# Shorter key blocks without the middle copy of the global keys, and another order of the first steps, in a banded attention with a gated MLP

## The chip, the cores and the metric

The kernel runs on one core of a Trainium2 chip. Its engines are TensorE (PE, with PEld for its weight loads), VectorE (DVE), ScalarE (ACT) and GpSimd (POOL); SyncE (SP) issues all DMAs of this kernel, in order. The metric is the device time of one execution in microseconds, as the median of several runs; durations come from one profiled execution.

## The reference

There are 8 batches of 8 heads, 512 local and 32 global tokens, 64 channels per head, all in float32. The output is cut to this:

```python
s_g = scale * q_g @ k_all.T                 # global tokens see every key
out_g = softmax(s_g) @ v_all
s_ll = where(abs(i - j) <= 32, scale * q_l @ k_l.T, -1e9)
s_l = concat([scale * q_l @ k_g.T, s_ll])   # local: 32 global keys and a band
out_l = softmax(s_l) @ concat([v_g, v_l])
x = rows of concat([out_g, out_l])          # 8 * 544 rows of 512
out = (((x @ w1) * (x @ w2)) @ w3) @ w_out  # no activation between
```

## The kernel before

**Attention.** Of a head's 512 queries, four blocks e of 128 are scored against a window of keys: `WIN` gives where a window begins in the loaded keys and how wide it is, `PAT` where its probabilities stand in the row `P` of the head (`PW` wide). In the loaded row of keys (`KD` = 608 wide) the 32 global keys g stand between the blocks of 128 local ones, three times: k0 g k1 g k2 g k3. A middle window (256 wide) holds 32 keys of the block before, g, 128 of its own, g again, and 32 of the next; one of the two g is masked out. Heads go in pairs: one head's keys lie in partitions 0 to 63 and the other's in 64 to 127, and `scores` issues their products alternately on the two halves of the array (a block's product shows as two matmuls in the trace). `scores1` does the heads 0 and 1 singly. `minus_max` adds the mask and takes the row minimum of the negated scores on DVE, `exps` the exponential on ACT.

**Two ways to turn the probabilities.** For heads 0 to 7 PE transposes them (`transposes`), ACT and DVE copy them into `PT` and `G`, and float32 products follow. From head 8 on DVE turns 32 by 32 squares (`turn` for the edges and global columns, `turn_own` for the own keys), and the squares are put in place through DRAM: `own_out` writes the tile `od`, `own_in` reads it back as `own` in four DMAs (there is one buffer for `own`, free again when the head before has been split), `weights_hi` rounds it into `PT` (ACT PT<-own) and `weights_lo` subtracts (PT<-own,PT). `move_out` and `move_in` do the same for the columns of G. Then `values` makes the products av with the values, in halves x.

**MLP.** The weights come packed, so that DVE (shift L841, merge L845) and ACT (scale L843) unpack them. w3 and w_out are first multiplied with each other on PE (`fold`, 8 times 8 products of 512 columns, L921 `w<-wo,w3f`), which makes w34. w1 and w2 are split into high and low parts; the second half of them, named w12s in the steps, comes in 16 pieces through three buffers, and a piece's fetch (SP L885) waits until the low part (DVE or POOL, `w12l`) of the piece three before it is made. `first` makes ap and bp (24 matmuls of 256 columns for two blocks m), `gate_a` copies ap out on ACT (`as`, L793), after which ap's one bank may be written again, `gate_b` multiplies on DVE, `second` adds to the output accumulators (acc, 6 matmuls per m).

**Order.** A list `PLAN` of some 3,880 entries gives every step's number and its engine (P, A, D, V for POOL, S); each engine works through its own entries in order and waits at the first whose inputs or buffers are not there. A few dummy products (`IDLE`) fill PE at the start.

Of the kernel before, what the change touches and what calls it, by code (L numbers as in the profile page):

```python
# [20 lines left out]
KD = 608  # L21
WIN = [(0, 192), (96, 256), (256, 256), (416, 192)]
PAT = [0, 192, 448, 704]
PW = 896
# [6 lines left out]
def i(ap):  # L31
# [8 lines left out]
    qgl=(250, 461), vgh=606, vgl=(620, 1290), mmax=(437, 502), exps=(545, 592), inv=350, mul=(420, 740),  # L40
    hi=(587, 231, 231, 475, 294, 203, 256), hi_dve=(683, 260, 260, 540, 0, 0, 292), lo=(692, 253, 253, 559, 540, 247, 280), half=(470, 530), sum=520, join=485,
# [4 lines left out]
    scores1=1650, scores2=1910, ownt=780, ownl=(691, 1300), values32=(1180, 1130), gscores32=930, take=(446, 521), shiftp=(330, 300, 420),  # L46
# [24 lines left out]
    1V 790S 386S 3V 328S 791S 0S 390S 329S 8S 12S 16S 389S 5V 387P 792P 152S 846S 388D 793D 391P 795D 794A 797D 796A  # L71
    392D 798A 9D 393A 799D 10A 394D 800A 11D 395P 14A 13D 801P 20S 396A 397A 15D 802D 24S 18A 813P 845S 803D 804D 17D
    19D 805A 808A 806A 248P 807V 814D 816D 28S 809P 815A 399S 817A 158S 818D 820D 811P 819A 821A 22A 21D 825P 830A 23D
    826D 249P 32S 164S 827A 829A 828A 847P 822D 832A 810D 26A 823S 25D 27D 36S 900S 831V 812D 30A 258P 868D 848D 850D
    833P 835P 849A 852D 854D 853A 851A 29D 31D 398S 250P 863A 855A 862V 870D 40S 872D 400P 403S 874D 34A 33D 856P 834A
    875A 251P 166A 873A 836D 35D 44S 857A 259P 260P 837D 859D 869A 858D 7V 401D 899S 261P 861A 38A 860D 37D 864P 866P
    39D 871A 48S 876D 877S 42A 165D 167D 41D 865A 879P 43D 886A 885A 404P 52S 880D 884A 881A 330S 883A 262P 405D 882A
    46A 2V 887P 45D 406A 47D 252P 888A 56S 407D 824S 901P 953S 50A 49D 253P 902D 51D 867A 889P 54A 53D 60S 331A 55D
    903A 159D 254P 922D 924D 58A 64S 57D 255P 256A 59D 263P 264P 265P 890A 68S 257D 268P 269P 923A 891V 402S 154A 839V
    904D 906D 892V 270P 908D 408P 160A 842V 266A 267D 333A 62A 61D 878S 909A 925A 271P 63D 272P 332D 72S 65D 66A 843A  # L80
    67D 409A 273P 926D 76S 410A 928D 70A 278P 69D 71D 929A 274P 907A 844D 80S 917A 275P 153D 412S 893V 279P 276D 277D
    954S 280P 74A 73D 281P 905A 75D 84S 927A 282P 896D 78A 910P 77D 930D 931S 283P 284P 912D 911A 79D 933P 915A 914A
# [12 lines left out]
    1031A 441D 1020A 1005A 1000V 419A 421A 3091P 1058D 1021V 420V 3095A 1057D 1114D 3093P 184A 422D 1229S 1061A 183D
    185D 1033S 172A 3092P 3094P 3101P 3102P 186A 171D 173D 178A 1059S 177D 1022A 187D 174A 179D 450S 1018A 175D 180A
    1084D 1085A 1086D 200S 1088D 1087A 188S 1116D 1115A 3096D 1089A 1062V 1065S 1019V 1023V 434S 1006V 3097A 1118D
    1034P 1037P 1060S 1120D 1090D 1035A 3103P 181V 3098D 202A 1038A 201D 1053V 1036D 1055A 194S 190A 3104P 1064V 1056V
    1039D 3105A 189D 191D 1091A 1066S 442P 203D 3111P 3106D 1156S 192A 1063A 1054V 1051A 1050S 193V 206S 1098D 451A
    1052D 3099P 204A 452V 1117A 1102A 1099D 196A 1067P 1070P 205D 1068A 1100S 3100P 218S 195D 197D 1094A 1071A 1103D  # L100
    198A 1095V 1069D 1106S 3113P 435A 199D 3107A 436V 1072D 212S 208A 3112P 3108D 437A 1101S 443A 207D 209D 1119A 3109P
    444D 438V 220A 1121A 219D 221D 1107S 1157P 210A 1122D 1104A 211V 1132D 1133S 1105A 1131D 1073V 1096A 222A 213D 214A
    3114P 224S 1135A 223D 1123S 3115A 215D 236S 1158D 1136V 1097V 3110P 1092A 1093V 1188D 216A 1190D 1139S 1159A 1160D
    1108P 217V 466S 1191A 3116D 1161A 1134S 3117A 1078V 1111P 1162D 1163A 1164D 1192D 3123P 3118D 226A 1194D 445S 1138A
    1165A 1137V 1140S 1109A 1112A 3121P 225D 237D 227D 228A 1075V 230S 1129A 229V 1172D 1176A 1110D 1113D 1127A 1177V
    242S 1173D 453P 454A 455D 1125A 1130V 1180S 1128V 238A 1174S 1126D 456A 1124S 239D 1141P 1144P 1189A 457D 458D
# [12 lines left out]
    3165P 1222V 486S 1293D 1328S 1323S 3166P 344A 1291D 473A 474V 1294D 1326A 1343A 1354D 1295V 3160D 1296V 3154P 475A
    1344D 1327A 1355S 1345S 494A 3161V 487S 1379P 3169A 1297D 3162V 3167P 1380D 1382D 1314V 1353D 3168P 1383A 1329S  # L120
    1315V 1410D 1381A 1412D 1357A 3163P 1414D 1411A 1416D 1298A 1358D 1318A 1299V 3179P 1384D 1361S 1386D 1385A 1227A
    1356S 1319V 3181P 345D 1316A 476D 3180P 3182P 1387A 1317V 3164P 1300V 1395D 504S 488S 495V 3170D 1301A 1396S 1330P
    1333P 1331A 3183P 3187A 1362S 1359V 1334D 1417A 1228D 3184P 1347V 1332D 3132S 3185P 3186P 1525S 3171A 1335D 1349A
# [161 lines left out]
def band_attention_glu_kernel(  # L285
# [20 lines left out]
    nc = tc.nc  # L306
# [6 lines left out]
    S = 544  # L313
# [12 lines left out]
    ident = cs[:, 0:128]  # L326
# [14 lines left out]

    def constants():
        nc.sync.dma_start(cs, cst)

    T = {}
    M = {}

# [180 lines left out]
    def transposes(n):  # L528
        P = Ps[n % NP_]
        tt = T["tt", n] = ps_1.tile([128, 2, 4, 128], F32, tag="pu", name=f"t{n}", bufs=2)  # L530
        for e in range(4):
            nc.tensor.transpose(tt[:, 0, e, :], P[:, 256 * e : 256 * e + 128], ident)
# [931 lines left out]
```

## Time and profile before

| | us |
|---|---|
| median of 3 runs (809.15 to 809.78) | 809.75 |
| the profiled execution | 809.29 |
| its span, first to last instruction | 807.5 |
| PE busy | 794.4 |
| DVE, ACT, POOL busy | 531.2, 455.3, 390.9 |
| PE in the chain that ended last | 94% of the span |

The page cuts the span in 40 slices; PE stands at 9 tenths or more in all but two of them, at about 117 and 147 us. A busy PE in this profile means that some matmul is in flight; since matmuls overlap, what one costs is read from how far apart they start, which is what the chain of work shows.

### The profile page before, as it was taken

Reading aid. Unit: us, or ns where it says so; the run is one execution under the profiler, and the core shown is the slowest. Engines: PE = TensorE matmul, PEld = TensorE weight load, DVE = VectorE, ACT = ScalarE, POOL = GpSimd, SP = SyncE. Lnnn points to the kernel's source line nnn. Section 1 sums busy time; section 2 is a strip of 40 time slices with the busy share of each in tenths; the row PEclk is TensorE's granted clock in tenths of the full one; section 3 lists DMA queues with packets and bytes.
Section 4 is the critical chain, followed back from the end, with each engine's and each line's share of the span. In section 5 each row is a group of like instructions: output and inputs, shape, how many; then the busy total and the mean of one; then the engine's idle time right before and its main releaser. Section 6 shows DMA issues by size and latency. Waiting matters only on the chain.

```text
span 807.5 us, 17227 instructions
## 1 busy us (share of the span) xinstructions
PE 794.4 (98%) x5608; PEld 704.6 (87%) x5608; DVE 531.2 (66%) x1504; ACT 455.3 (56%) x1290; POOL 390.9 (48%) x603
## 2 busy tenths in 40 slices
PE   9999989799999999999999999999999999999998
PEld 7656568699999999999999999999998999999997
DVE  4877978878777666677688867666576587612111
ACT  4767877776555545466665757665566554412011
POOL 1122354666555657656546556546556565412110
PEclk9999999999999999999999999999999999999999
DMA  8887877866557457565666656666664555300000
GB/s 275 266 267 226 262 193 193 207 171 187 160 151 206 122 155 180 144 188 138 162 174 170 202 157 169 177 171 173 187 171 130 137 152 153 97 27 14 15 27 26
DMA packets 191554, 128.85 MB, mean 160 GB/s; under 512 B 114472, under 2 KB 151592, under 8 KB 191464
## 3 DMA queue, kind: packets, MB, share of 16 engines
q1 hardware_dynamic: 191464, 127.75, 57.7%
q8 instruction: 44, 0.72, 0.4%
q14 instruction: 46, 0.38, 0.1%
HBM read 92.73 MB, written 34.96 MB: 158 GB/s over the span
## 4 chain that ended last, share of the span: by engine, by line
PE 94%; DVE 2%; ACT 1%; DMA 1%; SPq 1%; issue 0%; POOL 0%; ACTq 0%; DVEq 0%; POOLq 0%
PE bp L787 8%; PE ap L787 8%; PE acc L821 8%; PE acc L820 8%; PE acc L819 8%; PE bp L788 7%; PE bp L789 7%; PE ap L788 7%; PE ap L789 7%; PE w L921 7%; PE av L636 7%; PE s L491 6%; PE av L630 2%; PE sg L686 2%; DMA own<-od 1%; PE idle L364 1%
## 5 line engine op out<-in xcount | busy, mean ns | idle before, releaser
L787 PE MATMUL bp<-x,w12h 128*128 128x256 f32 x544 | 153.0, 281 | 0.0
L787 PE MATMUL ap<-x,w12h 128*128 128x256 f32 x544 | 152.5, 280 | 0.0
L788 PE MATMUL bp<-x,w12h 128*128 128x256 f32 x544 | 151.0, 278 | 0.0
L789 PE MATMUL bp<-x,w12l 128*128 128x256 f32 x544 | 150.8, 277 | 0.0
L788 PE MATMUL ap<-x,w12h 128*128 128x256 f32 x544 | 150.6, 277 | 0.0
L789 PE MATMUL ap<-x,w12l 128*128 128x256 f32 x544 | 150.5, 277 | 0.0
L504 ACT ACTIVATE P<-P,small 128x256 f32<-128x256 f32 (+1 forms) x256 | 121.6, 476 | 25.9 <-DVE small L500 25.1
L787 PEld LDWEIGHTS ap<-x,w12h 128*128 128x128 f32 x544 | 102.1, 188 | 4.0 <-issue 2.9
L787 PEld LDWEIGHTS bp<-x,w12h 128*128 128x128 f32 x544 | 102.6, 189 | 3.3 <-issue 2.2
L788 PEld LDWEIGHTS bp<-x,w12h 128*128 128x128 f32 x544 | 102.7, 189 | 0.7
L788 PEld LDWEIGHTS ap<-x,w12h 128*128 128x128 f32 x544 | 102.3, 188 | 0.7
L789 PEld LDWEIGHTS bp<-x,w12l 128*128 128x128 f32 x544 | 102.6, 189 | 0.0
L789 PEld LDWEIGHTS ap<-x,w12l 128*128 128x128 f32 x544 | 102.2, 188 | 0.0
L500 DVE CUSTOM_DVE_ANT_0 P<-s,cs 128x192 f32<-128x192 f32 (+1 forms) x256 | 86.1, 383 | 7.1 <-PE s L491 4.2
L650 DVE TENSOR_TENSOR u<-av,cb 64x352 f32<-64x352 f32 x112 | 55.7, 517 | 33.3 <-ACT cb L417 30.9
L417 ACT COPY cb<-av 64x352 f32<-64x352 f32 x71 | 30.6, 446 | 61.3 <-PE av L636 46.8
L636 PE MATMUL av<-PT,vs 128*128 128x192 f32 x448 | 62.0, 266 | 0.6 <-POOL PT L420 0.6
L921 PE MATMUL w<-wo,w3f 128*128 128x512 f32 x128 | 58.7, 597 | 0.3 <-DVE wo L845 0.3
L491 PEld LDWEIGHTS s<-kq,qp 64*128 64x128 f32 x496 | 43.3, 186 | 15.6 <-issue 6.5
L420 POOL TENSOR_TENSOR TT<-TT 128x352 fp32r<-128x352 f32 x38 | 38.5, 1013 | 35.7 <-ACT TT L417 20.5
L491 PE MATMUL s<-kq,qp 64*128 64x192 f32 (+1 forms) x496 | 55.4, 362 | 0.0
L636 PEld LDWEIGHTS av<-PT,vs 128*128 128x128 f32 x448 | 53.0, 164 | 2.7 <-POOL PT L420 0.8
(818 smaller groups left out, 1872.5 us busy)
## 6 DMA issues: line engine op xcount, KB each, us to landing
od<-tw SPq DMA_DIRECT2D x56, 256.0 KB, 2.6
own<-od SPq DMA_DIRECT2D x224, 64.0 KB, 2.4
raw_w<-in_w_t_dram SPq DMA_DIRECT2D x24, 512.0 KB, 4.9
kq<-in_kd_t_dram SPq DMA_DIRECT2D x32, 304.0 KB, 3.6
kpr<-in_kp_t_dram SPq DMA_DIRECT2D x32, 272.0 KB, 3.9
out_dram<-o_None SPq DMA_DIRECT2D x33, 256.0 KB, 2.8
qp<-in_q_t_dram SPq DMA_DIRECT2D x32, 256.0 KB, 3.7
R<-rd SPq DMA_DIRECT2D x64, 128.0 KB, 3.1
```

The source lines that it names most:

```text
L491: nc.tensor.matmul(st[:, x, c : c + w], q[r, 128 * e : 128 * e + 128], k[r, o : o + w], start=(e % 2 == 0), stop=True, skip_group_check=True)
L500: nc.vector.tensor_tensor_reduce(blk(n, e), s, masks[e], -0.125, 3.0e38, ALU.add, ALU.min, T["mn", n][:, e : e + 1])
L504: nc.scalar.activation(blk(n, e), blk(n, e), AF.Exp, bias=T["mn", n][:, e : e + 1], scale=-1.0, accum_out=T["sm", n // 2][:, n % 2, e : e ...
L636: nc.tensor.matmul(av[0:r, o : o + 32 * (s1 - s0)], v[:, 0:r], PT[:, s0:s1, y, j], start=False, stop=(j % 2 == 1 and (plain or y == 1)), s ...
L650: nc.vector.tensor_add(T["u", n // 2][r : r + 64, x], T.pop(("av", n, x))[r : r + 64, 0:352], T["cb", n][r : r + 64, x])
L787: nc.tensor.matmul(d, wh[:, k, c, :], x[:, 0, 0:w], start=(k == m % 2 == 0), stop=False, skip_group_check=True)
L788: nc.tensor.matmul(d, wh[:, k, c, :], x[:, 1, 0:w], start=False, stop=False, skip_group_check=True)
L789: nc.tensor.matmul(d, wl[:, k, c, :], x[:, 0, 0:w], start=False, stop=(k == 3), skip_group_check=True)
L819: nc.tensor.matmul(a, gh[:, m % 2, sl], wh[:, c], start=(m == 0), stop=False, **part)
L820: nc.tensor.matmul(a, gh[:, m % 2, sl], wl[:, c], start=False, stop=False, **part)
L821: nc.tensor.matmul(a, gl[:, m % 2, sl], wh[:, c], start=False, stop=(m in (5, 7)), **part)
L921: nc.tensor.matmul(T["w34", t], T["w3f", t, j // 4][:, j % 4], T["wo"][:, j], start=(j == 0), stop=(j == 7))
```

## The change

The keys are loaded without the copy of g between k1 and k2: k0 g k1 k2 g k3, in one DMA of two pieces of 288 columns. The windows become 192, 224, 224 and 192 wide, each with g once, at another place in the last two than in the first two. All that reads `P` follows: the columns of `transposes`, the squares of `turn` and `turn_own`, the pieces copied to G. The constant masks are the same array, in which a new step on POOL (`masks`, two copies of 128x32) exchanges two strips before the first masked block is read. In `values` the second of two value blocks takes its 64-column product first. The order of the first 1,378 of the 3,877 entries is new (to about head 16); the rest of the list is as it was.

```diff
-KD = 608
-WIN = [(0, 192), (96, 256), (256, 256), (416, 192)]
-PAT = [0, 192, 448, 704]
-PW = 896
+KD = 576
+WIN = [(0, 192), (96, 224), (256, 224), (384, 192)]
+PAT = [0, 192, 416, 640]
+PW = 832
...
-    1V 790S 386S 3V 328S 791S 0S 390S 329S 8S 12S 16S 389S 5V 387P 792P 152S 846S 388D 793D 391P 795D 794A 797D 796A
+    1V 790S 386S 328S 3V 387P 791S 792P 0S 3877V 388D 390S 793D 8S 391P 5V 794A 795D 392D 797D 799D 796A 393A 12S 800A
...
-    masks = [cs[:, 384:576], mask, mask, mask[:, 0:192]]
+    masks = [cs[:, 384:576], cs[:, 128:352], cs[:, 352:576], cs[:, 128:320]]
...
+    def order_masks():
+
+        nc.gpsimd.tensor_copy(cs[:, 320:352], cs[:, 352:384])
+        nc.gpsimd.tensor_copy(cs[:, 352:384], cs[:, 128:160])
...
-        nc.sync.dma_start(kr, kd_t[b, 2 * p : 2 * p + 2].rearrange("h d s -> (h d) s"))
+
+        k = kd_t[b, 2 * p : 2 * p + 2].rearrange("h d s -> (h d) s")
+        nc.sync.dma_start(kr.rearrange("p (a s) -> p a s", a=2), view(k, 0, [320, 2], [1, 288]))
...
-        nc.vector.transpose(view(t, 32, [256, 3], [64, 3], [1, 32]), view(P, 160, [32, 3], [256, 3], [1, 32]))
-        nc.vector.transpose(t[:, 7, 1], P[:, 128:160])
+        nc.vector.transpose(view(t, 32, [256, 2], [64, 3], [1, 32]), view(P, 160, [32, 2], [224, 3], [1, 32]))
+        nc.vector.transpose(view(t, 480, [64, 2], [128, 2], [1, 32]), view(P, 128, [96, 2], [448, 2], [1, 32]))
...
-            for y in range(1 if plain else 2):
+            ys = (0,) if plain else (1, 0) if j % 2 else (0, 1)
+            for y in ys:
...
-                [("s", n) if n < 2 else ("sp", n // 2), *([("mmax", n, e - 1)] if e else [("load", "cs")])], minus_max, n, e)
+                [("s", n) if n < 2 else ("sp", n // 2), *([("mmax", n, e - 1)] if e else [("masks",)])], minus_max, n, e)
...
+    add(("masks",), only("POOL", 200, True), -30.0, [("load", "cs")], order_masks)
```

**DVE, after the last fold.** Here DVE makes the last low part of w34 and then the low parts `w12l` of the first three w12s pieces. Before:

```order
L928 TENSOR_TENSOR w34l_998<-w_7_948,w34h_997 128x512
L658 COPY u_896<-av_7_989 64x352
L509 TENSOR_SCALAR sums<-sums 128x8
L510 RECIPROCAL sums<-sums 128x8
L420 TENSOR_TENSOR w12l_1016<-raw_w12s_2_266,w12h_1015 128x256
L420 TENSOR_TENSOR w12l_1016<-raw_w12s_0_150,w12h_1015 128x256
L662 TENSOR_TENSOR u_896<-u_896 128x32
L663 TENSOR_TENSOR u_896<-u_896 128x32
L526 TENSOR_TENSOR u_896<-u_896,R_951 128x256
L420 TENSOR_TENSOR w12l_1016<-raw_w12s_1_240,w12h_1015 128x256
```

The same place now:

```order
L936 TENSOR_TENSOR w34l_991<-w_7_911,w34h_990 128x512
L666 COPY u_890<-av_7_968 64x352
L426 TENSOR_TENSOR w12l_1002<-raw_w12s_2_638,w12h_1001 128x256
L426 TENSOR_TENSOR w12l_1002<-raw_w12s_0_185,w12h_1001 128x256
L426 TENSOR_TENSOR w12l_1002<-raw_w12s_1_206,w12h_1001 128x256
L426 TENSOR_TENSOR x_2_0_946<-u_665,x_2_0_946 128x256
```

The three low parts now follow each other, and the sums (`inverse`) and the work on u stand behind them.

**ACT, at the first copy of ap.** `as` is the copy that frees ap's bank; raw_w12s is a piece of weights just fetched, TT the turned edges of a head. Before:

```order
L417 CAST x_3_1_1098<-u_896 128x256
L417 CAST vs_1102<-vr_1006 128x4x64 x2
L793 COPY as__1119<-ap_0_0_1056 128x512
L843 ACTIVATE raw_w12s_1_1042<-raw_w12s_1_1042 128x256
L417 CAST TT<-TT 128x11x32
L843 ACTIVATE raw_w12s_3_1054<-raw_w12s_3_1054 128x256
```

And now:

```order
L423 CAST vs_1085<-vr_1034 128x4x64
L851 ACTIVATE raw_w12s_1_1037<-raw_w12s_1_1037 128x256
L423 CAST TT<-TT 128x11x32
L801 COPY as__1101<-ap_0_0_1054 128x512
L851 ACTIVATE raw_w12s_3_1040<-raw_w12s_3_1040 128x256
```

The copy has moved behind the scale of the first fetched piece and behind TT. On PE the second `first` of ap has moved the other way: before, 24 matmuls on bp stood between the first ap and the next, now 12 do, and the other 12 come after it, ahead of head 8's values.

**PE, ahead of head 11's values.** sg are scores of global queries, av the values, acc the accumulators. Before:

```order
L787 MATMUL ap_0_6_1560<-x_3_0_1075,w12h_1019 128x256
L788 MATMUL ap_0_6_1560<-x_3_0_1075,w12h_1019 128x256
L789 MATMUL ap_0_6_1560<-x_3_0_1075,w12l_1020 128x256
L686 MATMUL sg_1594<-kph_1318,QG_423 128x272 x2
L686 MATMUL sg_1594<-kpl_1330,QG_423 128x272 x2
L630 MATMUL av_1616<-G_1039,vgs 128x288
```

And now:

```order
L694 MATMUL sg_1570<-kph_1309,QG_420 128x272 x2
L694 MATMUL sg_1570<-kpl_1358,QG_420 128x272 x2
L827 MATMUL acc_0_0_1299<-w34h_779,gh__1529 128x512
L828 MATMUL acc_0_0_1299<-w34l_780,gh__1529 128x512
L829 MATMUL acc_0_0_1299<-w34h_779,gl__1546 128x512
L827 MATMUL acc_0_128_1300<-w34h_779,gh__1529 128x512
L828 MATMUL acc_0_128_1300<-w34l_780,gh__1529 128x512
```

One `second` (6 matmuls) that stood behind head 11's values now stands ahead of them; 12 matmuls of a `first` have changed places with the global scores.

## Rows read from the trace of the kernel before

**Rows 1.** The page, part 1: busy time, share, instructions of each engine.

```profile
PE 794.4 (98%) x5608; PEld 704.6 (87%) x5608; DVE 531.2 (66%) x1504; ACT 455.3 (56%) x1290; POOL 390.9 (48%) x603
```

**Rows 2.** Windows: length, busy PE, PEld, DVE, ACT, POOL, granted clock, DMA, GB/s.

```profile
105.00:125.00 20.00, 17.21 (x127) 16.18 (x126) 14.91 (x47) 14.72 (x43) 11.54 (x16) 0.91 0.84 203
...
140.00:160.00 20.00, 15.21 (x100) 12.86 (x99) 17.01 (x57) 15.52 (x46) 13.88 (x24) 0.91 0.87 213
...
200.00:300.00 100.00, 100.00 (x759) 92.74 (x758) 71.15 (x198) 54.46 (x161) 57.15 (x89) 1.00 0.60 161
```

**Rows 3.** PE's waits over the span: us in total, times, longest.

```profile
PE av L630 <- DVE small L717: 3.8, 1, 3.8
PE av L630 <- ACT P L504: 2.8, 1, 2.8
...
PE av L636 <- POOL PT L420: 0.6, 1, 0.6
PE av L630 <- ACT w12h L417: 0.4, 1, 0.4
```

**Rows 4.** The chain that ended last: start, us, what.

```profile
7.46 1.71 PE s L476 x8
...
79.18 6.87 PE w L921 x16
...
155.88 1.72 PE s L491 x16
```

**Rows 5.** Groups by form: count, busy us, mean ns of one.

```profile
L636 PE MATMUL av<-PT,vs 128*128 128x224 f32 x112 | 31.3, 280 | 0.0
...
L636 PE MATMUL av<-PT,vs 128*64 128x224 f32 x112 | 30.3, 270 | 0.0
```

**Rows 6.** The chain from the last fold to head 8's values.

```profile
105.95 0.60 DVE w34l L928
...
107.23 0.39 DVE sums L509
...
109.27 0.34 DVE w12l L420
...
109.63 0.33 SPq L885
...
110.05 0.97 SPq L556
...
112.78 5.26 DMA own<-od
...
118.14 0.62 ACT PT L417
...
120.48 0.40 PE av L630
```

**Rows 7.** DVE in order of time, 100 to 134 us.

```profile
107.77 0.71 DVE L420 TENSOR_TENSOR w12l<-raw_w12s,w12h 128x256 fp32r<-128x256 f32 x2
...
127.35 0.65 DVE L420 TENSOR_TENSOR PT<-own,PT 128x512 fp32r<-128x512 f32 x1
...
131.75 0.53 DVE L650 TENSOR_TENSOR u<-av,cb 64x352 f32<-64x352 f32 x1 [1.06 <-ACT cb L417]
132.31 0.43 DVE L420 TENSOR_TENSOR w12l<-raw_w12s,w12h 128x256 fp32r<-128x256 f32 x1
```

**Rows 8.** POOL in order of time, 118 to 121 us.

```profile
118.83 1.27 POOL L420 TENSOR_TENSOR PT<-own,PT 128x512 fp32r<-128x512 f32 x1 [2.55 <-ACT PT L417]
120.18 0.24 POOL L420 TENSOR_TENSOR G<-TGg,G 32x32 fp32r<-32x32 f32 x1
```

**Rows 9.** ACT in order of time, 112 to 115 us.

```profile
112.29 0.59 ACT L793 COPY as__1119<-ap 128x512 f32<-128x512 f32 x1 [0.36 <-PE ap L789]
114.45 0.45 ACT L843 ACTIVATE raw_w12s<-raw_w12s 128x256 f32<-128x256 f32 x1 [1.57 <-DMA raw_w12s<-in_w_t_dram]
114.79 0.47 ACT L417 CAST TT<-TT 128x352 fp32r<-128x352 f32 x1
```

**Rows 10.** Tile bp, 108 to 117.5 us: ns min/median/max, first and last start.

```profile
L787 PE MATMUL bp<-x,w12h x8: 276/276/276, 112.1 to 114.5; 128*128 128x256 f32 x8
```

**Rows 11.** The chain at a `second`, one of its six.

```profile
128.02 0.23 PE acc L819
```

**Rows 12.** SP's waits over the span.

```profile
SPq L885 <- DVE w12l L420: 6.2, 4, 3.2
```

More of the change, by code (lines that the diff above doesn't have):

```diff
@@ L39 @@
     kh=703, kl=(790, 1500), qh=617, ql=(620, 1290), vh=404, vl=(545, 746), kph=647, kpl=(726, 1374), qgh=298,
-    qgl=(250, 461), vgh=606, vgl=(620, 1290), mmax=(437, 502), exps=(545, 592), inv=350, mul=(420, 740),
-    hi=(587, 231, 231, 475, 294, 203, 256), hi_dve=(683, 260, 260, 540, 0, 0, 292), lo=(692, 253, 253, 559, 540, 247, 280), half=(470, 530), sum=520, join=485,
+    qgl=(250, 461), vgh=606, vgl=(620, 1290), mmax=(437, 470), exps=(545, 568), inv=350, mul=(420, 740),
+    hi=(587, 231, 231, 366, 294, 203, 366), hi_dve=(683, 260, 260, 416, 0, 0, 416), lo=(692, 253, 253, 559, 540, 247, 280), half=(470, 530), sum=520, join=485,
     joing=750, xh=405, xl=(411, 740), cg=610, mg=790, eg=840, ng=820, wg=(683, 292), ga=588, gb=691, gh=620,
@@ L45 @@
     gtrans=465, own=355, turn=650, gturn=1010, edge=(513, 520), edgel=(520, 960), first=1372, second=1382, fold=860,
-    scores1=1650, scores2=1910, ownt=780, ownl=(691, 1300), values32=(1180, 1130), gscores32=930, take=(446, 521), shiftp=(330, 300, 420),
+    scores1=1543, scores2=1610, ownt=780, ownl=(691, 1300), values32=(1180, 1130), gscores32=930, take=(446, 521), shiftp=(330, 300, 420),
 )
@@ new lines @@
+    430D 132A 952D 973A 431D 133V 1009P 1010D 140S 136A 318P 313P 135D 1012D 137D 314P 993V 315P 1014D 1155S 975A 141D
+    146S 319P 167D 142A 1011A 432S 138A 1082S 1015A 1040D 1013A 320P 148A 1016D 321P 439S 1042D 948A 316A 139V 1081S
+    322P 147D 1230S 323P 149D 143D 317D 324P 150A 1017A 325P 1024D 995P 986S 1044D 1025D 151V 144A 145V 1041A 1028A
+    433S 326A 1029V 1046D 1043A 327D 168A 1026S 1032S 162A 997P 156V 996D 6V 1083P 169D 418S 157D 182S 163D 170S 4V
+    998A 949D 1047A 440A 999D 1045A 1022A 1001D 3087P 1002A 1031A 176S 1030A 441D 1023V 1020A 3089P 1058D 419A 1003V
@@ new lines @@
+    184A 3088P 1084D 1057D 1061A 1004V 183D 3090P 3095A 1027S 1059S 1033S 1048D 185D 171D 1062D 172A 173D 1114D 3091P
+    3092P 3101P 186A 1005A 187V 1086D 1116D 174A 421A 1018A 175V 1021V 1118D 1088D 420V 1120D 1065S 200S 3102P 188S
+    1117A 1087A 1019D 3093P 178A 1049S 1119A 3094P 1085A 177D 1229S 179D 1006V 3096D 1090D 1115A 1089A 1034P 180V 1037P
+    201D 1035A 3097A 3103P 181D 189D 1038A 1036D 1060S 422V 3104P 1064V 190A 1039D 1063A 194S 1091A 191D 1055A 450S
+    3098D 1053A 1000V 1099D 1098D 442P 1056V 192A 1054V 1066S 202A 1051A 193D 195D 1052D 3105A 3099P 196A 1102A 451A
@@ new lines @@
+    1379P 3162D 1328S 474D 1297V 1327A 3170D 495V 1380D 3179P 3181P 3163P 1298A 1382D 1381A 1227A 1315D 1355S 1384D
+    1299V 3164P 1386D 1353D 487S 1410D 1357A 1329S 475A 3171A 1412D 345V 1318A 1316A 1358V 1300D 1383A 1387A 1319V
+    1385A 1317V 3183P 1228D 3172D 1395D 1356S 3180P 3185P 3182P 1414D 3187A 1296V 1330P 1333P 3132S 3173P 1351A 1331A
+    3193P 1332D 1359V 3184P 1361S 1411A 1360V 1396S 1334A 3186P 1394D 476V 1362S 1398A 1349A 3194P 1415A 488S 1347V
+    1416D 1352D 1348D 1350V 1345S 1301A 1335D 496P 1399V 3188D 1417A 1363P 1366P 1451S 3174P 3195P 1364D 1413A 3197A
@@ new lines @@
+    1365D 1452S 1402S 1367A 1368D 1400A 1397S 1390A 504S 1302V 497A 3189A 489A 1428D 1401V 3177A 3175A 498D 1429S 1391D
+    1392A 490V 1427D 1431A 1526S 3203P 1403S 491A 3190D 1346S 1393D 1418D 1453P 1454D 1388A 1432V 3204P 1484D 505A
+    1455A 3196P 1456D 1486D 346S 1457A 1458D 1488D 1389V 1460D 1461A 3198D 492V 3191P 1404P 1459A 1487A 1407P 1435S
+    506V 1369V 1405A 1490D 3205P 1469D 1408A 507P 1406D 1419S 1423A 1409D 3192P 1425A 3207A 1371V 1374D 3206P 508A
+    1375A 1430S 3213P 1485A 1433V 1470S 1434V 1424V 1436S 1421A 3199A 509D 1525S 510A 1426V 1468D 1422D 3200D 499S 511D
@@ new lines @@
+    1437P 1489A 1472A 1420S 1471S 1372A 512D 1473V 3214P 1491A 1440P 1438D 1441A 513S 1502D 1439D 1442D 500V 1443V
+    3201P 3208D 1475V 1476S 1474A 3202P 1527P 1492D 1528D 501V 3215P 1462A 1445V 1503S 1501D 1530D 3217A 347A 514S
+    3216P 1532D 1558D 3209A 1505A 3210V 1463V 1506V 1464V 1466A 3218D 1534D 1560D 1467D 3227P 1373D 1562D 3228P 3211P
+    1564D 1370V 1531A 1477S 1493S 3212P 1535A 3231A 1504S 1448D 1509S 1465V 1376D 1533A 348V 1529A 1543D 3178S 520S
+    1494S 1478P 3219V 1481P 1479D 1510S 1508D 3220V 1480D 1499A 1482D 502A 1544S 3176S 349A 3229P 1507A 3230P 1495A
@@ L137 @@
+    503V 1483D 1542D 1561A 1446A 1500V 3221P 515S 1497A 521A 1496D 3232D 1599S 531S 1559A 3222P 1498D 522D 1511P 1546A
+    1449A 1547D 1514P 3225D 3233V 3234V 1550S 3237P 1545S 1512D 1513D 1600S 1540A 1565A 1515A 1538A 3238P 350D 523P
     1673S 1516D 1548A 3226S 3223D 1517V 3241A 3239P 1551S 1450D 1519V 1563A 532A 1549A 516V 518V 1576D 3240P 1536V 524A
@@ L326, in band_attention_glu_kernel @@
     ident = cs[:, 0:128]
-    mask = cs[:, 128:384]
-    masks = [cs[:, 384:576], mask, mask, mask[:, 0:192]]
+    masks = [cs[:, 384:576], cs[:, 128:352], cs[:, 352:576], cs[:, 128:320]]
     Ps = [const.tile([128, PW], F32, tag=f"P{e}", name=f"P{e}") for e in range(NP_)]
@@ L530, in transposes @@
         tt = T["tt", n] = ps_1.tile([128, 2, 4, 128], F32, tag="pu", name=f"t{n}", bufs=2)
-        for e in range(4):
-            nc.tensor.transpose(tt[:, 0, e, :], P[:, 256 * e : 256 * e + 128], ident)
-        for e in range(3):
-            nc.tensor.transpose(tt[:, 1, e, :], P[:, 256 * e + 128 : 256 * e + 256], ident)
+        for e, c in enumerate((0, 256, 448, 704)):
+            nc.tensor.transpose(tt[:, 0, e, :], P[:, c : c + 128], ident)
+        for e, c in enumerate((128, 352, 576)):
+            nc.tensor.transpose(tt[:, 1, e, :], P[:, c : c + 128], ident)
     def turn(n):
         P, t = Ps[n % NP_][:], f(TT[:])
-        nc.vector.transpose(view(t, 32, [256, 3], [64, 3], [1, 32]), view(P, 160, [32, 3], [256, 3], [1, 32]))
-        nc.vector.transpose(t[:, 7, 1], P[:, 128:160])
+        nc.vector.transpose(view(t, 32, [256, 2], [64, 3], [1, 32]), view(P, 160, [32, 2], [224, 3], [1, 32]))
+        nc.vector.transpose(view(t, 480, [64, 2], [128, 2], [1, 32]), view(P, 128, [96, 2], [448, 2], [1, 32]))
     def turn_own(n):
@@ L545, in turn_own @@
         t = T["tw", n] = p1.tile([128, 512], F32, tag="tw", name=f"tw{n}")
-        nc.vector.transpose(view(t[:], 0, [32, 4], [128, 4], [1, 32]), view(P, 0, [256, 4], [32, 4], [1, 32]))
+        nc.vector.transpose(view(t[:], 0, [64, 2], [32, 2], [128, 4], [1, 32]), view(P, 0, [448, 2], [256, 2], [32, 4], [1, 32]))
     def own_out(n):
@@ L597, in pieces @@
         tt = T["tt", n]
+        g_own = G[0:32, 32:S].rearrange("g (c d x) -> g c d x", c=2, d=2)
         if e == 0:
```

109 lines of the change are left out of this document (41 added, 68 removed).

## The prediction

> **What bounds the kernel now.** I read the busy times first: PE is busy for 794.4 of 807.5 us, the next engine, DVE, for 531.2 [rows 1]. The windows say where the rest is: from 200 to 300 us PE is busy in 100 of 100 us at full clock while DVE has 29 us to spare [rows 2], so there only PE's own work counts. [...] The waits name the places: PE stands 2.8 us ahead of head 8's values, 1.0 us around head 10's and 3.8 us ahead of head 11's [rows 3]. So up to 7.6 us of standing and 3.6 us of lost clock lie within the stretch whose order is new, and everywhere else the kernel is as long as PE's matmuls. The last view is the chain, for what a matmul costs and for who is late at those places.
>
> **Part 1, narrower score blocks.** 16 fold matmuls of 512 columns take 6.87 us in the chain [rows 4], 0.84 ns a column. The score matmuls of a pair of heads are 8 steps, the two heads side by side: 4 steps of 192 and 4 of 256 columns, 1,792 columns, 1.50 us by that price; the chain has 1.72 [rows 4], the rest being the ends. Now the four wide steps have 224 columns: 4 x 32 x 0.84 ns = 0.107 us less. There are 31 such pairs, and the heads 0 and 1, scored singly with the same 8 steps each (1.71 us [rows 4]), save as much each: 33 x 0.107 = 3.5 us, nearly all of it where PE never waits, or ahead of a chain that starts on PE. Ends of the price: 0 if the steps are not set by columns (a rival below), 3.5 if they are; I take 3.5, since the fold row prices a column.
>
> The trace shows both heads' 16 matmuls in 1.72 us and one head's 8 in 1.71 [rows 4]: twice the weight loads, the same time. [...]
>
> **Part 2, the order at head 8.** The chain there [rows 6, 7]: the last low part of w34 at 105.95, the sums at 107.23, two low parts w12l (0.71 us from 107.77), a third at 109.27, by which the third fetch leaves at 109.63 and the read-back of head 8's own keys only at 110.05; it lands at 118.04, is rounded on ACT at 118.14 (0.62), and its low part takes POOL 1.27 us, with G's 0.24 behind it [rows 8]. In the new order the three low parts follow each other: 107.23 + 0.71 + 0.34 = 108.28 instead of 109.61, 1.3 us earlier for the read-back. The low part of the own keys goes to DVE, 0.65 us [rows 7], with G's part done before: 118.76 + 0.65 = 119.4 instead of 120.4, 1.0 less. Seven score blocks ahead of it take off 0.75. So the operands stand at 120.5 - 1.3 - 1.0 - 0.75 = 117.4, and PE comes at 117.7 - 0.75 = 116.9: this wait shrinks to about 0.5 us.
>
> What is late next is the copy that frees ap's bank. It ran at 112.29, ahead of the scale of the first fetched piece, which waited for its DMA until 114.45 [rows 9]. Now it stands behind that scale (0.45) and TT's rounding (0.47). The first fetch can leave 0.6 us earlier (the sums no longer ahead) and all is 0.75 earlier, so the piece lands at about 113.1, and the copy ends near 113.1 + 0.8 + 0.6 = 114.5. PE wants the bank after 12 instead of 24 matmuls on bp, which run from 112.1 to 114.6 [rows 10]: at 113.35 - 0.75 = 112.6. It would stand 1.9 us there, then has 36 matmuls left (4.1 us at the pace of rows 10) and is at head 8's values at 118.6 instead of 120.5. Behind the copy on ACT stand the next piece's scale and, five steps on, head 8's rounding; at 114.5 that still waits for its data. Gain 1.9, of which 0.75 is in part 1: 1.2 us. Ends: -1 if the piece lands no earlier, +2.4 if the copy isn't late.
>
> **Part 3, the order at heads 10 and 11.** The read-back of head 10 waits for a fetch, and that for a low part at 132.31, which stood behind a sum that waited 1.06 us and took 0.53 [rows 7]. The new order puts this low part first: 1.6 us earlier, and the one buffer of `own` hands that on to head 11. One `second`, six matmuls of 0.23 us [rows 11], now runs ahead of head 11's values, 1.4 us of work where PE stood 3.8. Together 3.0 us at most. Against it: a low part of the gate that this `second` needs has gone from DVE to POOL, which for the same 512 columns takes 1.27 against 0.65 us [rows 7, 8], and PE arrives earlier than before while DMA is at 0.87 [rows 2]. I take half, 1.5 us; ends 0 and 3.0.
>
> **Part 4, the clock.** Two drops, 1.8 us each. With the first long stand cut in two shorter ones I take one of them away: 1.8 us; ends 0 and 3.6.
>
> **What costs nothing.** The two mask copies on POOL (0.24 us is the nearest row, a quarter of their size [rows 8]) lie behind a load and ahead of an idle POOL, while PE runs dummy products; uncovered they cost 0.5 to 2 us once. A key load is 16 KB smaller in two pieces; it is issued long before its use. Narrower rows on DVE and ACT, and the regrouped turns, shorten engines that are not the bound; in the steady stretch DVE's spare 29 us cover them. In `values`, the 64-column matmul takes 270 ns and the 128-column one 280 [rows 5]; 112 halves with two exchanged are worth at most 1.1 us either way, taken as 0.
>
> **Sum.** 3.5 + 1.2 + 1.5 + 1.8 = 8.0. The profiled execution is 809.29 us, its span and 1.8 us around it; 809.29 - 8.0 = 801.3. The median of the runs lies 0.46 above it: 801.8 us.
>
> **Rivals.**
> The waits only change places: the 1.9 us at ap's bank and a late gate part give back what heads 8 and 11 gain, and both drops stay. For it: DVE and ACT are busy about three quarters of both stretches and DMA at 0.84 and 0.87 [rows 2], so there is little room to come earlier. Against it: the three low parts and the `second` move work out of the late chain itself. Only part 1 is left: 809.75 - 3.5 = 806.2.
> All waits close: 3.5, with most of the 7.6 and the 3.6 gone: 809.75 - 13.5 = 796.3. For it: the walk at head 8 leaves 0.5 us. Against: ap's bank.
> Score steps paced by their weight loads, 8 equal steps of 0.215 us, which fits the 1.72 just as well [rows 4]; then the change doesn't shorten PE, and 4.5 of the order is left: 805.3. Against it: the single heads' row.
> Slower: SP works in order, and three fetches stand ahead of each read-back; a fetch has waited up to 3.2 us for its buffer [rows 12]. If the new order holds up the read-backs of heads 10 and 11 that way, PE loses 6.4 us, less the 3.5 of part 1: 812.7. It decides from 5.1 us of new waiting on. For it: the hand-over through one buffer adds such delays up. Against it: each low part named above has moved forward.
>
> **How the numbers follow.** My forecast 0.57, waits change places 0.22, all close 0.10, paced by loads 0.05, slower 0.06. The likeliest one's own range is 799 to 804.5. To 807.5 the range takes in the cases at 805.3 and 806.2; below it goes to 798, since all that the new stretch could give lies at 796; outside are the slower case, most of the closing one and thin tails, about 2 in 10. A measurement tells 0.2% (1.6 us) from no change. Faster by more, under 808.1: the first four without a tail of the second and fourth, 0.89. Within: 0.06. Slower: 0.05.
>
> **What would show it.** Part 1: a pair's scores at 1.61 us in the chain, its four wide steps 27 ns shorter each. Part 2: a PE wait on the copy of ap near 112 us, and head 8's values at about 118.6. Part 3: the wait ahead of head 11's values under 2 us. Part 4: one of the windows 105 to 125 and 140 to 160 at clock 1.00. Wrong it is if the scores stay at 1.72, if a new wait of 3 us or more stands before 105 us, or if heads 12 to 15 wait in their turn.

## The result and the profile after

The changed kernel takes 818.21 us (816.43 to 818.62); beside it on the same chip the kernel before took 809.45 (807.72 to 809.78). The ratio is 1.0108 (1.0087 to 1.0129): 8.8 us slower, where 8 us faster was forecast. Its profiled execution took 816.43 us, 7.1 more than the one of before. What was worked out for the places that the change touches is nearly all there; what is lost, is lost in matmuls that the change doesn't touch.

Part 1 of the page after, then windows as in [rows 2]: length, busy PE, PEld, DVE, ACT, POOL, granted clock, DMA, GB/s.

```profile
PE 803.0 (99%) x5608; PEld 713.7 (88%) x5608; DVE 523.5 (64%) x1498; ACT 456.7 (56%) x1300; POOL 394.0 (48%) x601
```

```profile
0.00:50.00 50.00, 47.83 (x213) 33.26 (x214) 32.46 (x107) 29.86 (x85) 5.88 (x13) 1.00 0.85 267
50.00:105.00 55.00, 53.72 (x199) 30.27 (x198) 42.06 (x114) 40.04 (x107) 17.18 (x27) 1.00 0.76 236
...
105.00:125.00 20.00, 19.18 (x144) 17.26 (x143) 17.60 (x55) 17.41 (x55) 14.59 (x21) 1.00 0.78 208
...
140.00:160.00 20.00, 17.52 (x130) 15.24 (x130) 17.57 (x50) 14.56 (x40) 11.02 (x19) 1.00 0.62 177
...
600.00:800.00 200.00, 200.00 (x1462) 186.77 (x1461) 87.75 (x230) 73.67 (x198) 77.48 (x116) 1.00 0.30 83
```

PE's longest waits after (in all, times, longest), and a single head's and a pair's scores in the chain:

```profile
PE s L497 <- ACT PT L423: 1.3, 1, 1.3
...
PE s L497 <- DVE u L658: 0.9, 1, 0.9
PE bp L795 <- DVE g__1204 L805: 0.8, 1, 0.8
PE bp L795 <- DVE g__1356 L805: 0.8, 1, 0.8
PE av L644 <- DVE small L724: 0.7, 1, 0.7
```

```profile
7.46 1.60 PE s L482 x8
...
216.19 1.61 PE s L497 x16
```

A pair's scores take 1.61 us [rows 4: 1.72]; instead of the waits of 3.8 and 2.8 us [rows 3] there are several of at most 1.3; and both windows with the lost clock are at 1.00 [rows 2]. Yet the last window says that something else got worse. There PE is busy all the time at full clock, as it was before, and does fewer matmuls in 200 us: 1,462, where the kernel before did

```profile
600.00:800.00 200.00, 200.00 (x1489) 186.80 (x1488) 87.62 (x228) 73.47 (x194) 76.70 (x113) 1.00 0.29 81
```

1.8% more, of the same program but for its scores and `values`. After 677 us no score and after 708 us no `values` start in the changed kernel, and the loss goes on. The timeline has the starts: twelve products of `first`, from the first of one block to the first of the next, before and after (start, us, engine, line, what):

```profile
713.15 0.28 PE L787 MATMUL bp<-x,w12h 128*128 128x256 f32 x1
...
714.51 0.28 PE L787 MATMUL ap<-x,w12h 128*128 128x256 f32 x1
```

```profile
720.32 0.28 PE L795 MATMUL ap<-x,w12h 128*128 128x256 f32 x1
...
721.74 0.28 PE L795 MATMUL bp<-x,w12h 128*128 128x256 f32 x1
```

1.36 us and 1.42 us: 113.3 and 118.3 ns from start to start, with no wait, the same operands, the same clock. The duration shown for one product is 0.28 both times; it is the distance of the starts that changed. It isn't a spread but two paces. Call a row of `first` products with no other matmul between them a stretch, and a stretch fast where its last five distances are under 115 ns on average. Of the 3,264 products of `first`, all but 9 are in fast stretches before and 36 after; the fast ones stand at 113 to 114 ns, the slow ones at 117 to 119.

Adding up the distances from each matmul's start to the next by what the matmul is (waits taken out, us):

| | before | after |
|---|---|---|
| `first` (L787 to L789; L795 to L797) | 376.9 | 388.4 |
| `second` (L819 to L821; L827 to L829) | 189.7 | 191.3 |
| scores | 56.6 | 53.1 |
| `values`, products with PT | 57.3 | 56.5 |
| `values`, products with G | 21.8 | 22.2 |
| first to last start, waits included | 802.3 | 809.1 |

Scores gave 3.5 as forecast; standing and the clock gave about 2.4 of the 4.5 forecast; `first` and `second` took 13.1.

### The profile page after: what moved, and what is told of

It reads as the page before. It is cut to its first block, busy times and chain, and to the rows that moved or that the text cites. A ratio compares the mean times of both kernels' runs of the same rounds, so it can differ in the third digit from the quotient of the medians.

```text
span 814.6 us, 17157 instructions
## 1 busy us (share of the span) xinstructions
PE 803.0 (99%) x5608; PEld 713.7 (88%) x5608; DVE 523.5 (64%) x1498; ACT 456.7 (56%) x1300; POOL 394.0 (48%) x601
## 4 chain that ended last, share of the span: by engine, by line
PE 88%; DVE 4%; DMA 4%; issue 2%; ACT 1%; POOL 1%; DVEq 0%; ACTq 0%; POOLq 0%
PE bp L795 8%; PE ap L795 8%; PE bp L797 8%; PE bp L796 8%; PE ap L797 8%; PE acc L827 8%; PE acc L829 8%; PE acc L828 7%; PE ap L796 7%; PE av L644 6%; PE s L497 5%; PE av L637 2%; PE w L929 2%; DMA raw_w<-in_w_t_dram 2%; PE sg L694 1%
## 5 line engine op out<-in xcount | busy, mean ns | idle before, releaser
L795 PE MATMUL bp<-x,w12h 128*128 128x256 f32 x544 | 153.7, 283 | 1.6 <-DVE g__1204 L805 0.8
L795 PE MATMUL ap<-x,w12h 128*128 128x256 f32 x544 | 154.1, 283 | 0.0
L797 PE MATMUL ap<-x,w12l 128*128 128x256 f32 x544 | 152.1, 280 | 0.4 <-DVE w12l L426 0.4
L797 PE MATMUL bp<-x,w12l 128*128 128x256 f32 x544 | 152.0, 279 | 0.0
L510 ACT ACTIVATE P<-P,small 128x224 f32<-128x224 f32 (+1 forms) x256 | 118.7, 465 | 24.1 <-DVE small L506 23.4
L795 PEld LDWEIGHTS bp<-x,w12h 128*128 128x128 f32 x544 | 102.1, 188 | 5.0 <-issue 1.8
L795 PEld LDWEIGHTS ap<-x,w12h 128*128 128x128 f32 x544 | 102.0, 188 | 4.6 <-issue 2.9
L797 PEld LDWEIGHTS ap<-x,w12l 128*128 128x128 f32 x544 | 102.1, 188 | 0.6 <-DVE w12l L426 0.6
L797 PEld LDWEIGHTS bp<-x,w12l 128*128 128x128 f32 x544 | 102.1, 188 | 0.0
L506 DVE CUSTOM_DVE_ANT_0 P<-s,cs 128x192 f32<-128x192 f32 (+1 forms) x256 | 82.8, 365 | 6.0 <-PE s L497 3.7
L644 PEld LDWEIGHTS av<-PT,vs 128*128 128x128 f32 x448 | 57.0, 162 | 3.5 <-issue 0.8
L497 PE MATMUL s<-kq,qp 64*128 64x192 f32 (+1 forms) x496 | 52.5, 350 | 2.2 <-ACT PT L423 1.3
```

The lines of the kernel that those rows point to most:

```text
L497: nc.tensor.matmul(st[:, x, c : c + w], q[r, 128 * e : 128 * e + 128], k[r, o : o + w], start=(e % 2 == 0), stop=True, skip_group_check=True)
L506: nc.vector.tensor_tensor_reduce(blk(n, e), s, masks[e], -0.125, 3.0e38, ALU.add, ALU.min, T["mn", n][:, e : e + 1])
L510: nc.scalar.activation(blk(n, e), blk(n, e), AF.Exp, bias=T["mn", n][:, e : e + 1], scale=-1.0, accum_out=T["sm", n // 2][:, n % 2, e : e ...
L644: nc.tensor.matmul(av[0:r, o : o + 32 * (s1 - s0)], v[:, 0:r], PT[:, s0:s1, y, j], start=False, stop=(j % 2 == 1 and y == ys[-1]), skip_gr ...
L795: nc.tensor.matmul(d, wh[:, k, c, :], x[:, 0, 0:w], start=(k == m % 2 == 0), stop=False, skip_group_check=True)
L797: nc.tensor.matmul(d, wl[:, k, c, :], x[:, 0, 0:w], start=False, stop=(k == 3), skip_group_check=True)
```

## The experiments

What in the change could reach `first`, of which it moves nothing after entry 1,378? Two things. Smaller tiles: `P` is 64 columns narrower (two tiles), `kr` 32 (three), so all that is allocated behind them lies lower, x and w34 by 512 bytes, w12 by 896. And the exchange in `values`, which changes what stands ahead of a stretch of `first`. Theory A was the addresses; rival B the order or the narrower blocks.

**Addresses.** Three variants of the changed kernel with old tile sizes, of which the added columns stay unused, and the kernel before with an unused tile.

```diff
-    Ps = [const.tile([128, PW], F32, ...
+    Ps = [const.tile([128, 896], F32, ...          # first and second run
-        kr = p2.tile([128, KD], F32, tag="kr", ...
+        kr = p2.tile([128, 608], F32, tag="kr", ... # first and third run, kpr too
```

```diff
+    p1q.tile([128, 32], F32, tag="pad", name="pad") # kernel before, fourth run
     sums = p1q.tile([128, 2, 2, 4], F32, tag="sums", name="sums")
```

> The changed kernel, but the tiles of P keep 896 columns and the tiles of K keep 608, of which the last 64 and 32 stay unused: every instruction and its order are those of the changed kernel, and only the addresses in SBUF of what is allocated behind these tiles move back (x by 512 bytes, w12 by 896). Theory A (the 3,264 products of L795 to L797 follow each other every 117.8 ns and not every 113.9 because of where their operands lie): spacing back to 114 ns, 3,264 x 3.9 = 12.7 us and about 2 us in L827 to L829 come off 816.4, so 801 to 804 us. Rival B (the new order or the narrower score blocks slow the products): spacing stays at 118 ns and the time at 816 to 819 us.

> As the last one, but only the tiles of P keep their old size: x and w34 lie where they lay in the kernel before, w12 lies 384 bytes lower than there. Theory A, if the place of x and w34 decides: 801 to 804 us, products of the first stage at 114 ns. If the place of w12, or its distance from x, decides: 114 ns only by luck, about 815 us. Rival B: 816 to 819 us.

> As the first one, but only the tiles of K keep their old size: x and w34 lie 512 bytes lower than in the kernel before, as in the changed one, w12 lies 512 bytes lower too, so that the distance between w12 and x is that of the kernel before. Theory A, if the distance between the two operands decides (modulo a few hundred bytes): 801 to 804 us; if the place of x alone: 815 to 818 us. Rival B: 816 to 819 us.

> The kernel before with an unused tile of 128 bytes ahead of the tiles of K, so that w12 and everything behind it lie 128 bytes higher; every instruction is that of the kernel before. By its last nine address bits each operand of the first stage then lies as in the changed kernel. Theory A, if the place of w12 or its distance from x decides: the spacing rises from 113.9 to about 118 ns and the time to 820 to 823 us. Rival B (order or narrower blocks are the cause), or if the place of w34 and x decides: 809 to 810 us, no change.

The kernel before took 809.94 there. Measured: 813.69 (ratio 1.0044, 1.0025 to 1.0063); 819.82 (1.0125, 1.0085 to 1.0164); 813.62 (1.0046, 1.0025 to 1.0066); 820.65 (1.0134, 1.0097 to 1.0171). The fourth decides: the instructions of the kernel before, one tile of 128 bytes put in, 10.7 us slower, and all 3,264 products at the slow pace. Its window shows it as the changed kernel's did:

```profile
600.00:800.00 200.00, 200.00 (x1463) 186.69 (x1462) 90.19 (x236) 76.85 (x207) 78.54 (x118) 1.00 0.32 87
```

So no order and no block width is needed for the loss. The second and third tell that it is the distance between w12 and x that counts, not the place of x. But the first, with all at its old place, came to 813.7 and not to 801 to 804: theory A alone falls short. Its trace shows both paces in one kernel, 3.9 us apart, with the same four x tiles. Ahead of the first block stand scores and another block, ahead of the second `values`:

```profile
611.00 0.28 PE L795 MATMUL ap<-x,w12h 128*128 128x256 f32 x1
...
612.36 0.39 PE L827 MATMUL acc<-w34h,gh__8203 128*128 128x512 f32 x1
...
614.38 0.57 PE L644 MATMUL av<-PT,vs 128*128 128x224 f32 x4
...
614.93 0.28 PE L796 MATMUL bp<-x,w12h 128*128 128x256 f32 x1
...
616.11 0.28 PE L797 MATMUL bp<-x,w12l 128*128 128x256 f32 x1
```

Twelve starts in 1.36 us, 113 ns; then ten in 1.18, 118 ns. Of the stretches that follow `values` 41 of 48 are slow there, of those that follow scores 2 of 25. Once it has settled, a pace is kept to the end of the stretch: in none of the seventeen traces of this study does a stretch of more than twelve products, behind 160 us, change its pace after its first seven distances. It does not start at once: in the kernel before, the stretches behind `second` begin with some five distances of 116 to 123 ns and then run at 113 to 114. And `second` hands it on: in the four runs that have both paces in plenty (first, third, sixth and thirteenth), two stretches with only `second` between them have the same pace 106 times of 108, while all 52 slow stretches with `second` and scores behind them are followed by a fast one.

**The exchange in `values`.** The first run's kernel with the old order in `values`; the kernel before with the new one; the changed kernel with the old one; and the kernel before with its unused tile placed so that x moves with w12.

```diff
-            ys = (0,) if plain else (1, 0) if j % 2 else (0, 1)
+            ys = (0,) if plain else (0, 1)          # fifth and seventh run
```

```diff
+    const.tile([128, 32], F32, tag="pad", name="pad") # kernel before, eighth run
     TT = const.tile([128, 11, 2, 32], F32R, tag="TT", name="TT")
```

> The first run's kernel (changed kernel, tiles of P and K at their old sizes), and in values the 128-column product of each half first again, so that a head's last product has 64 columns as in the kernel before. Theory: the products of the first stage have two paces, 113.5 and 118 ns; which one a stretch gets is set as it begins; with w12 at its new place it is always the slow one, with w12 at its old place only behind values that end with a 128-column product. Then all stretches run at 113.5 to 114 here, 1,545 x 4.3 ns = 6.6 us and about 1 us of second come off the 813.7 of the first run: 805 to 807 us. Rival (the order of the steps, not the last product of values, sets the slow pace): 812 to 815 us.

> The kernel before, only with the new order in values (the second half's 64-column product first). Theory: w12 lies at its old place, but the stretches behind values begin at 118 ns and keep it, about half of all: 809.9 + 6.6 + 1 = 816 to 818 us less about 1 us if the exchanged products themselves are shorter. Rival (the exchange is worth nothing or a gain): 808 to 811 us.

> The changed kernel with the old order in values, its tiles at their new sizes. Theory: with w12 at its new place all stretches are at 118 ns whatever stands ahead of them: 817 to 821 us, no gain. Rival (the order in values alone is the cause): 805 to 808 us.

> The kernel before with the unused 128 bytes placed ahead of TT, so that x, w34 and w12 all lie 128 bytes higher. If the place of w12 by itself decides (an address that is not a multiple of 256 is the good one): 118 ns, 819 to 822 us as with w12 alone moved. If the distance between w12 and x decides: 113.5 to 114 ns, 809 to 811 us.

The kernel before: 809.03. Measured: 806.62 (0.9966, 0.9948 to 0.9984); 817.18 (1.0089, 1.0056 to 1.0122); 819.60 (1.0129, 1.0096 to 1.0161); 809.55 (1.0000, 0.9983 to 1.0016). All four came out as the theory had it. Products in fast stretches: 3,123; 1,608; 72; 3,207. So there are two causes, and either is enough: the exchange alone costs the kernel before 8.2 us, the addresses alone 10.7, and with both undone the changed kernel is faster than the kernel before. The eighth run shows that w12 may lie where it was bad in the fourth if x lies 128 bytes higher too.

**Distance, and the order by itself.** On the fifth run's kernel an unused tile of 64 or 96 columns ahead of `sums`, as in the fourth run; and the fifth run's kernel with the entries of the old order.

```diff
-    1V 790S 386S 328S 3V 387P 791S 792P 0S 3877V 388D ...
+    1V 790S 386S 3V 328S 791S 0S 3877V 390S 329S 8S ...   # eleventh run: old list, with the new step
```

> The kernel of the fifth run (changed kernel, old tile sizes, old order in values) with an unused tile of 256 bytes ahead of the tiles of K: w12 lies 256 bytes further from x than there. Theory: the pace hangs on the distance between the two operands modulo some hundreds of bytes (+128 was bad, +0 and both +128 good). If modulo 256: +256 is good again, 806 to 807 us; if modulo 512, it may be either: 118 ns and 817 to 820 us, or 113.5 ns and 806.

> As the last one with 384 bytes. If the pace goes by the distance modulo 256: bad, 118 ns, 817 to 820 us. If modulo 512: open, 806 or 818 us; a pace below 113 ns, 800 us or less, would show that neither of the two seen so far is the best.

> The kernel of the fifth run with the old order of the first 1,378 entries (the step that exchanges the mask strips put in behind the load of the constants): what is left of the change are the narrower score blocks. Theory of the prediction: part 1 is worth 3.5 us, so 0.9957 of the kernel before, 805.5 us where that takes 809.0; and the order is worth up to 4.5 us, which the fifth run (0.9966) does not show, so this run and the fifth tell what the order brings on this chip: if 804 to 806.5 us here, the order brings nothing; if 809 or more, the order brought what the fifth run gained.

The kernel before: 809.54. Measured: 806.43 (0.9960, 0.9940 to 0.9980); 820.29 (1.0130, 1.0101 to 1.0159); 806.14 (0.9967, 0.9949 to 0.9984). The pace goes by the distance modulo 256 bytes: counted from the places that the tiles got, w12 minus x is 64 there in the kernel before and in all runs that were not slow for it, 192 in the changed kernel and in the second, fourth, seventh and tenth run. Other tiles, those of K among them, move along with w12 in these runs; that it is w12 and x is concluded from the slow products, which read nothing else.

The old order is as fast as the new one, as far as ratios with an interval of 0.002 either way can tell: the narrower blocks bring the whole gain, 3.4 us here. The windows of the eleventh run, and of the ninth, which has the new order:

```profile
0.00:50.00 50.00, 48.28 (x214) 33.44 (x215) 33.78 (x109) 31.16 (x88) 8.69 (x21) 1.00 0.89 274
50.00:105.00 55.00, 55.00 (x204) 31.22 (x203) 45.67 (x118) 41.45 (x111) 15.43 (x21) 1.00 0.80 240
105.00:160.00 55.00, 47.53 (x355) 43.60 (x354) 45.92 (x138) 43.52 (x131) 32.09 (x50) 0.97 0.79 201
```

```profile
0.00:50.00 50.00, 46.15 (x203) 31.92 (x204) 30.53 (x101) 27.68 (x77) 4.87 (x12) 1.00 0.83 255
50.00:105.00 55.00, 53.99 (x204) 31.16 (x203) 42.07 (x116) 39.80 (x108) 17.21 (x26) 1.00 0.77 229
105.00:160.00 55.00, 50.58 (x346) 42.48 (x345) 46.21 (x135) 45.19 (x130) 33.08 (x49) 1.00 0.79 210
```

The new order wins 3.05 us of PE's time between 105 and 160 us, and the clock; it loses 2.13 ahead of 50 us and 1.01 up to 105. These windows tell where the time goes and not what the order is worth: the two profiled executions took 804.16 us (eleventh) and 807.18 (ninth), while the medians lie 0.3 apart. Most of the 2.13 is one wait, for wo:

```profile
PE w L930 <- DVE wo L854: 1.8, 1, 1.8
```

It was 0.2 us in the changed kernel's own profile and 0.9 to 2.2 in the seven profiles of the new order taken in these studies, 0.3 in all with the old one. Why that start is so much more sensitive was not tried.

**A rule for other operands?**

```diff
             W34[t] = tuple(const.tile(...) ...)
+            if t == 7:
+                const.tile([128, 32], F32, tag="pad", name="pad")   # twelfth and fourteenth run;
+                                                                   # two more such tiles ahead of G (or vs) and sums
-            ys = (0,) if plain else (0, 1)
+            ys = (0,) if plain else (0, 1) if j % 2 else (1, 0)     # thirteenth run
+    p1q.tile([128, 16], F32, tag="padq", name="padq")               # fifteenth run, ahead of sums
```

> The kernel of the eleventh run (narrow score blocks, old order, old tile sizes, old order in values) with three unused tiles of 128 bytes: gh and gl then lie 128 bytes further from w34, and w12 256 bytes further from x, vgs and G likewise, which the ninth run showed to be harmless. In L827 to L829 the distance from moving operand to weights, 192 bytes modulo 256 until now, becomes the 64 that w12 and x have. Theory (a general rule): L828 and L829, now every 227.3 and 229.4 ns, come to the 225 of L827, some 2 us off 806.1: 803.5 to 805. Rival (peculiar to w12 and x): 805.5 to 807 us, the three spacings as they were.

> The kernel of the eleventh run, with the exchange in values made in the first value block of a half and not in the second: 64, 128, 128, 64 columns. Theory: the product that stands last decides the pace behind it, so the first stage stays at 114 ns; if the equal neighbours are as short as in the changed kernel (97.5 ns on average for 102), up to 1.5 us less than 806.1: 804.5 to 806. Rival (any exchange brings the slow pace): 811 to 814 us.

> As the first run of this set, with vs another 128 bytes further from PT, so that in values too the distance is 64 bytes modulo 256. Theory (a general rule): values, 448 products of 96 to 105 ns, lose a few ns each, 1 to 3 us beside the first run of this set: 801 to 804 us. Rival: like the first run of this set.

> The kernel of the eleventh run with w12 64 bytes further from x, halfway between the good distance and the bad one. Two levels only: 114 ns and 806 us, or 118 ns and 817 to 819 us. A third level in between (116 ns, about 812 us) would speak for a cost that grows with the distance.

The kernel before: 810.57. Measured: 808.11 (0.9975, 0.9959 to 0.9992); 815.22 (1.0050, 1.0034 to 1.0066); 808.84 (0.9970, 0.9959 to 0.9982); 822.18 (1.0143, 1.0111 to 1.0174). The general rule fell: at the distance that is good for `first`, `second` is slower. Three of its products, from one L829 to the next (L832 in the twelfth run), in the eleventh and in the twelfth run:

```profile
699.54 0.39 PE L829 MATMUL acc<-w34h,gl__9658 128*128 128x512 f32 x1
...
700.23 0.39 PE L829 MATMUL acc<-w34h,gl__9658 128*128 128x512 f32 x1
```

```profile
704.62 0.40 PE L832 MATMUL acc<-w34h,gl__9661 128*128 128x512 f32 x1
...
705.32 0.39 PE L832 MATMUL acc<-w34h,gl__9661 128*128 128x512 f32 x1
```

230 and 233 ns a product; over all threes of neighbours behind 160 us the medians are 229 and 233. So the two pairs of operands that were tried don't share a good distance; the ratios of the eleventh and twelfth run (0.9967, 0.9975) don't tell the difference. The thirteenth run refutes my reading that the product that stands last decides: 64 columns last, and 47 of 49 stretches behind `values` slow. Both departures from the old sequence of widths did it. Whether `values` itself hands a pace on is not shown: its products with 128-column weights take 111 to 112 ns from start to start in the thirteenth run and 105 in the eleventh, but 103 in the changed kernel, where nearly every stretch is slow. `values` gains nothing that can be told in the fourteenth run. And 64 bytes more (128 modulo 256) are a little worse than 128 more (192): the starts within stretches behind 160 us lie 120.0 ns apart on average, against 118.9 in the seventh and tenth run. That is a third pace, not between the other two but beyond them, so the cost doesn't simply grow with the distance from the good place.

## Why the prediction was wrong

The step that failed is "What costs nothing". It priced the reordered `values` by its own products only (1.1 us either way, taken as 0) and the narrower keys and rows by the engines that touch them. It took for granted, without saying so, that a matmul which the change leaves alone keeps its pace. That pace, 113.5 ns, was itself read from a row [rows 10], and treated as a property of the shape. What the runs showed in its place: it hangs on where w12 lies against x (10.7 us by that alone, fourth run) and on the order in `values` ahead (8.2 us by that alone, sixth run). 3,264 products times 3.5 ns, by the table 11.5 us, and 1.6 in `second`, are the terms the sum lacked; no rival held them either. The slower rival (read-backs on SP, 812.7) was another mechanism, and waits of its size are not in the profile after.

Part 1 was right: 1.61 us a pair, 56.6 to 53.1 us over the 33 blocks of scores, and 3.4 us in the eleventh run, where little else is changed. With that the rival of steps paced by their weight loads is out.

Parts 2 and 3 closed the waits that they named: between 104 and 240 us nothing longer than 0.9 us is left where 2.8 and 3.8 stood. But in part 2 the mechanism was wrong and its time near by luck. Head 8's values start at 119.1 (before 120.5, forecast 118.6), yet the wait of 1.9 us on the copy of ap that was to make them so late is not there; PE is busy from 105 us up to them. Without that wait the forecast would have been 116.7. Of the 2.4 us from there to 119.1, 1.7 is standing further ahead, since PE is busy for 101.55 us up to 105 after and for 103.28 before (the rest was not traced):

```profile
0.00:50.00 50.00, 48.28 (x213) 33.44 (x214) 33.61 (x108) 30.53 (x86) 8.24 (x19) 1.00 0.89 274
50.00:105.00 55.00, 55.00 (x202) 31.05 (x201) 46.24 (x120) 41.85 (x111) 15.86 (x21) 1.00 0.79 243
```

So standing moved ahead of 105 us, in pieces that each stay under the 3 us I had named as a warning. That is the rival "the waits only change places", in a stretch that the parts on the order leave out. The profile after still shows 2.4 us gained, with 0.2 us of waiting for wo; the ninth against the eleventh run show that over several executions the order is worth nothing that can be measured.

Part 4 was right and too small: both drops are gone in the profile, and in ten runs of the ninth kernel the mean granted clock was 0.999 to 1.000, against 0.991 to 0.998 in those of the kernel before beside them. In the ninth kernel the new waits take that back as well. Its 1.8 us a drop, and the 3.6 us of lost clock, can be worked out from [rows 2] alone, 20 us at 0.91 in each window. Finer windows of the trace before have the clock at 0.50 for some 3.4 us each time, from 120.8 and from 151.5 us, and at 1.00 on either side of it; by estimate that is 1.7 us of full-speed work a drop:

```profile
118.00:120.00 2.00, 0.00 (x0) 0.00 (x0) 2.00 (x10) 1.86 (x7) 1.17 (x1) 1.00 1.09 307
120.00:122.00 2.00, 1.52 (x8) 1.52 (x9) 1.49 (x8) 1.47 (x6) 1.79 (x4) 0.69 0.88 298
122.00:124.00 2.00, 2.00 (x12) 2.00 (x11) 0.91 (x3) 1.37 (x5) 0.74 (x3) 0.50 1.10 285
```

That a shorter stand of PE spares a drop was my estimate, and no run shows it: in the eleventh the clock is 0.91 between 105 and 125 us, where PE stands 3.0 us, and 1.00 between 140 and 160 us, where it stands 3.3.

Why the distance of two operands modulo 256 bytes sets a pace is open; no run shows what lies behind it. The fourth and eighth run, which differ only in where the unused tile stands, and so in whether x moves along with w12, show that it does: 820.65 and 809.55 us.

## What to carry to other kernels

Changing a tile's size moves the tiles behind it (here one unused tile of 128 bytes moved w12 and cost 10.7 us, fourth run): where a kernel is bound by PE, compare the distance between the starts of untouched matmuls before anything else, and if it changed, put the old size back. Where a stretch has two paces, the products ahead of it are part of its cost, so reordering a handful of them can cost more than they take (8.2 us in the sixth run, for products priced at 1.1 us at most). A wait that closes in one window is a gain only if the windows ahead of it stay full (here PE stood 1.7 us more ahead of 105 us).

## What was not expected of the hardware

- Products of 128x128 by 256 columns follow each other every 113.5 or every 118 ns at the same granted clock of 1.00 (120 at one more distance), and keep a pace, once settled, through stretches of up to 93 products and through `second` between them (106 times of 108).
- w12 minus x modulo 256 bytes: 64 gives the fast pace (four different placings), 192 the slow one (820.3 and 820.7 us for the kernel), 128 a slightly slower one still (822.2); 0 was not tried. For 512 columns of w34 against gh, 192 is better than 64: 229 against 233 ns in the median.
- At the good distance the sequence of widths in `values` still decides: 128, 64, 128, 64 leads to the fast pace (3,123 of the 3,264 products in the fifth run), 128, 64, 64, 128 and 64, 128, 128, 64 to the slow one behind nearly all of them (41 of 48 stretches in the first run, 47 of 49 in the thirteenth).
